# Windowed attention and a squared-ReLU MLP on one core: attention in pairs of PSUM banks, group 0's down-projection by products, merged stores, and a new order

## The chip, the cores and the metric

The kernel runs on one core of one Trainium2 chip. The metric is the time of one launch on the device in microseconds (us), the median of several runs of the same program. Engines are called as in the profile: PE (TensorE, matrix products), PEld (its weight loads, which run beside it), DVE (VectorE), ACT (ScalarE), POOL (GpSimd, which here only issues the loads) and SP (SyncE, which here only issues transfers). PSUM has eight banks of 128 x 512 float32.

## The reference

```python
def _attn_ref(q, k, v):                    # each (8, 8, 576, 64): batch, head, position, head size
    scores = scale * np.matmul(q, k.transpose(0, 1, 3, 2))
    rel = pos[:, None] - pos[None, :]
    slopes = 2.0 ** (-8.0 * (np.arange(H) + 1) / H)
    bias = slopes[:, None, None] * (-np.abs(rel))[None]
    mask = (rel >= 0) & (rel < 128)
    scores = np.where(mask, scores + bias[None], -1000000000.0)
    attn = softmax(scores)
    return np.matmul(attn, v)

x = attn_out.transpose(0, 2, 1, 3).reshape(4608, 512)
h = x @ w_in                               # (512, 2048)
r = np.maximum(h, 0.0)
return (r * r) @ w_out                     # (2048, 512), float32
```

So a query sees itself and at most 127 keys before it. The two matrix products of the MLP are nearly all of the arithmetic.

## The kernel before, in words

**Tokens.** The 4608 tokens are nine groups of 512 (g = 0 to 8). A group is made of four ranges of 128 tokens; a range is a block of 128 positions of one batch entry or, since 576 = 4 x 128 + 64, a pair of 64-token blocks of two batch entries. The order of the blocks is fixed in `seq` and `ranges`; the first eight blocks are the first blocks of the eight batch entries.

**Attention of a block m.** POOL issues the loads of k, q and v (128 KB each as they land in bf16, L522 and L527). k and q are transposed, by PE for the first eight blocks (L583), by a transfer issued on SP for the others (`kqT`, L568). PE makes the scores (task `s`, L642) into four PSUM banks of the ring "a". ACT takes the exponential of each bank (`e`, L669, 512 columns), DVE multiplies each by a table of exp(bias) with the mask in it (`m`, L677, L680, L684). PE multiplies by v (`pv`, L749) in two halves of four heads, each half in one bank of the same ring "a"; a column of ones beside v gives the sum of the row. DVE takes the reciprocal (`r`, L768) and multiplies (`n`, L777), for each half. The result is transposed into xT, by PE for the first eight blocks (L797), by a transfer on SP for the others (L784). The first four blocks (`lone`) add the bias by a matrix product with an identity instead (L697, L706) and have two exponentials of 512 (L714).

**MLP up.** For groups 0 to 5, PE makes h in pieces of one PSUM bank of the ring "h" (two banks): tasks `u` (L896) in groups 0 to 2 and `fc` (L914) in groups 3 to 5. A piece of group 0 is four feature blocks of 128 by 128 tokens, and there are four such sets, one for each range of tokens; the set of features names the part of w_in that it needs. Groups 6 to 8 use seven products of 256 columns instead of eight (task `f`, L995, Strassen's method in Winograd's form). ACT takes the ReLU into a ring "rt" (L857), DVE or ACT squares it into the bf16 tile g (L869, L867).

**MLP down.** Group 0 is done directly: for each range of 128 tokens, 16 matmuls of 512 columns (task `o`, L1071), evacuated by ACT or DVE and stored as 128 x 512. Groups 1 to 8 go by seven products of half size instead of eight (`product`, task `p` g.number.half, L1158): products 1 and 2 need only g and w_out; 5 and 6 need sums of quarters of g (`S1`, `S2`, made by DVE at L1281 out of the finished g) and of w_out (`wsum`, made once at L1114); 7, 3 and 4 need `S3` and `S4`. A group's four results are snapped or added into SBUF tiles "osb" (L376, L374, L1212, L1221, L1224) and stored by SP, each 128-token quarter-result by a transfer of its own (L1196), a pair of 64-token blocks by two. The last product of group 8 is cut up at the very end (`last_product`, L1241, L1251, L1258).

**The order.** All of it is tasks with a key (when it is wanted), candidate engines, dependencies, and rings of buffers that they take and give back. `Plan.order` lays them out once, when the program is built, with a table of costs, and every engine then runs its instructions in that fixed order; `ADJ` holds corrections of single keys. Where the plan foresees a gap on PE in the first 30 us, `fill` (L355) puts dummy matmuls there. The weights are loaded in pieces between the first blocks' loads (`FIRST`, w_in in five pieces of 2, 2, 4, 4 and 4 feature blocks, w_out in four).

Of the kernel before, what the change touches and what calls it, by code (L numbers as in the profile page):

```python
# [22 lines left out]
N_PVH = 2  # L23
# [15 lines left out]
G_STR = 1  # L39
G_A = 8  # L40
XR = 12
OSB = 5
# [6 lines left out]
RT = 4  # L49
# [80 lines left out]

class Slot:


    def __init__(self, tag):
        self.tag, self.tile, self.left, self.freed, self.idx, self.turn = tag, None, 0, 0.0, 0, 0


class Plan:


    LAT = {"PE": 210.0, "ACT": 180.0, "DVE": 190.0, "POOL": 200.0, "SP": 200.0, "ACTQ": 200.0}
    SELF = {"ACT": 120.0, "DVE": 110.0}
# [123 lines left out]
def kernel(  # L266
# [23 lines left out]
    for b in range(0, B, 2):  # L290
        for x in [(b + i, kb) for i in range(2) for kb in range(1, HALF)]:
            jobs.append(("full", [len(seq)]))
            seq.append(x)
            ranges.append([x])
        jobs.append(("half", [len(seq), len(seq) + 1]))
        seq += [(b, HALF), (b + 1, HALF)]

        ranges.insert(len(ranges) - (b + 2 == B), seq[-2:])
# [58 lines left out]
    def tile_of(slot):  # L357
        return tiles[slot.tag][slot.idx]

    def act(n):  # L360
        return n * 0.832 + 51.0
# [980 lines left out]
```

## Time and profile before

| | us |
|---|---|
| three runs | 301.82, 301.49, 300.56 |
| median of the runs | 301.49 |
| the profiled execution | 302.54 |
| its span (first to last instruction) | 300.8 |
| what lies around the span | 1.74 |
| PE busy / DVE / ACT / POOL | 288.8 / 243.3 / 205.2 / 106.5 |
| mean granted clock of PE | 0.994 |

The span is what the profile's rows add up to; the profiled execution is 1.05 us above the median of the runs. Busy times of one engine don't add up with another's: they run side by side. In the chain that ended last, PE has 85% of the span, a transfer of w_in 5%, POOL's issuing 5%, DVE 2%.

### The profile page before, as it was taken

How to read it: one execution, taken by the hardware profiler on the slowest of the kernel's cores; microseconds unless marked ns; L12 is line 12 of the kernel's file. 1: busy time of each engine (PE TensorE's matmuls, PEld its weight loads, DVE VectorE, ACT ScalarE, POOL GpSimd, SP SyncE). 2: the span in 40 equal slices, each digit the busy share in tenths (PEclk: the TensorE clock that was granted, in tenths of full speed). 3: DMA queues.
4: the chain of work that ended last, by engine and by line, in shares of the span. 5: the costliest groups of instructions: out<-in, count | busy, mean ns of one | idle time of the engine just before them, and what ended most of it. 6: DMA issues, size and time to landing. Idle time of an engine off the chain costs nothing.

```text
span 300.8 us, 8326 instructions
## 1 busy us (share of the span) xinstructions
PE 288.8 (96%) x3279; PEld 226.2 (75%) x3299; DVE 243.3 (81%) x628; ACT 205.2 (68%) x390; POOL 106.5 (35%) x132
## 2 busy tenths in 40 slices
PE   8799999997999999999999999999999999999992
PEld 4588757886888888556576776568888888888882
DVE  5567568679877899688799997699989998999852
ACT  2685445576487673785978747896979669888710
POOL 8944488445551585522639205510000000000000
PEclk9999999999799999999999999999999999999999
DMA  9999999999999999999999999996103101110213
GB/s 126 170 201 206 181 190 159 164 173 174 174 167 186 123 130 187 164 157 140 167 187 179 160 191 166 152 158 107 37 17 109 38 35 37 70 37 0 80 61 108
DMA packets 170920, 39.62 MB, mean 132 GB/s; under 512 B 156928, under 2 KB 170368, under 8 KB 170880
## 3 DMA queue, kind: packets, MB, share of 16 engines
q0 software_dynamic: 115184, 18.10, 86.5%
q1 hardware_dynamic: 55264, 20.66, 39.2%
q8 instruction: 26, 0.43, 0.6%
q10 hardware_dynamic: 432, 0.33, 0.4%
q14 instruction: 14, 0.11, 0.1%
HBM read 36.70 MB, written 9.44 MB: 153 GB/s over the span
## 4 chain that ended last, share of the span: by engine, by line
PE 85%; DMA 5%; POOL 5%; DVE 2%; issue 1%; POOLq 0%
PE o L1158 33%; PE h L914 14%; PE h L995 12%; PE h L896 10%; PE pv L749 6%; PE s L642 5%; DMA w_in_sb<-in_moe_w_in_dram 5%; PE o L1071 4%; POOL kq L522 2%; POOL vf L527 1%; POOL w_in_sb L467 1%; DVE sums L1281 1%; PE tp L583 1%; PE o L1241 1%; DVE g L869 1%
## 5 line engine op out<-in xcount | busy, mean ns | idle before, releaser
L857 ACT ACTIVATE rt<-h 128x512 bf16<-128x512 f32 (+1 forms) x109 | 64.4, 595 | 30.6 <-PE h L896 14.8
L669 ACT ACTIVATE P<-s 128x512 bf16<-128x512 f32 x120 | 63.6, 604 | 12.7 <-PE s L642 12.7
L1158 PEld LDWEIGHTS <-g 128*128 128x128 bf16 x624 | 59.5, 98 | 8.2
L869 DVE TENSOR_TENSOR g<-rt 128x512 bf16<-128x512 bf16 (+1 forms) x101 | 41.7, 415 | 20.1 <-ACT rt L857 18.6
L522 POOL DMA_DIRECT2D kq<-in_k_dram x39 | 33.2, 852 | 54.0 <-DMA kqT<-kq 47.4
L1158 PE MATMUL o<-w_out_sb,g 128*128 128x256 bf16 x384 | 47.2, 273 | 0.0
L896 PE MATMUL h<-xT,w_in_sb 128*128 128x128 bf16 (+1 forms) x512 | 46.6, 246 | 0.4 <-DMA w_in_sb<-in_moe_w_in_dram 0.4
L914 PE MATMUL h<-xT,w_in_sb 128*128 128x512 bf16 x178 | 45.0, 379 | 0.7
L896 PEld LDWEIGHTS <-w_in_sb 128*128 128x128 bf16 x512 | 38.6, 98 | 4.2 <-DMA w_in_sb<-in_moe_w_in_dram 0.6
L677 DVE TENSOR_TENSOR P<-P,masks 128x512 bf16<-128x512 bf16 x96 | 38.3, 416 | 3.1 <-ACT P L669 1.2
L527 POOL DMA_DIRECT2D vt<-in_v_dram x32 | 27.1, 855 | 31.5 <-PE pv L749 30.7
L522 POOL DMA_DIRECT2D kq<-in_q_dram x39 | 33.6, 862 | 7.7 <-PE h L896 3.2
L1158 PE MATMUL o<-wsum,sums 128*128 128x256 bf16 x256 | 32.9, 279 | 2.1 <-DVE sums L1281 2.1
L777 DVE TENSOR_TENSOR x<-pv,rec 128x256 bf16<-128x256 f32 (+1 forms) x80 | 31.7, 413 | 0.7
L1158 PE MATMUL o<-wsum,g 128*128 128x256 bf16 x240 | 30.7, 273 | 0.0
L1158 PEld LDWEIGHTS <-sums 128*128 128x128 bf16 x256 | 25.1, 100 | 6.6 <-DVE sums L1281 2.3
L914 PEld LDWEIGHTS <-w_in_sb 128*128 128x128 bf16 x192 | 17.2, 98 | 16.6
L749 PEld LDWEIGHTS <-P 128*128 128x128 bf16 (+1 forms) x576 | 23.7, 101 | 6.2 <-issue 0.9
L867 ACT ACTIVATE g<-rt 128x512 bf16<-128x512 bf16 x44 | 27.6, 629 | 1.1
L857 ACT ACTIVATE rt<-vf 128x512 bf16<-128x512 f32 x36 | 22.5, 626 | 6.2 <-DVE vf L1016 5.8
L1016 DVE TENSOR_TENSOR vf<-h,vf 128x512 f32<-128x512 f32 x36 | 24.2, 685 | 2.6 <-PE h L995 2.2
L376 ACT ACTIVATE osb<-o 128x512 f32<-128x512 f32 x21 | 12.6, 598 | 17.1 <-PE o L1158 14.8
(81 smaller groups left out, 393.5 us busy)
## 6 DMA issues: line engine op xcount, KB each, us to landing
out_dram<-osb SPq DMA_DIRECT2D x55, 128.0 KB, 2.7
kq<-in_k_dram POOLq DMA_DIRECT2D x31, 128.0 KB, 7.0
kq<-in_q_dram POOLq DMA_DIRECT2D x31, 128.0 KB, 7.5
vt<-in_v_dram POOLq DMA_DIRECT2D x24, 128.0 KB, 7.5
w_out_sb<-in_moe_w_out_dram POOLq DMA_DIRECT2D x4, 512.0 KB, 14.6
w_in_sb<-in_moe_w_in_dram POOLq DMA_DIRECT2D x3, 512.0 KB, 10.6
out_dram<-osb SPq DMA_DIRECT2D x17, 64.0 KB, 2.1
vf<-in_v_dram POOLq DMA_DIRECT2D x8, 128.0 KB, 6.9
```

The lines of the kernel that those rows point to most:

```text
L522: nc.gpsimd.dma_start(view(kq[s_kq[m].idx], i), source(src, m, split))
L527: nc.gpsimd.dma_start(tile_of(s_v[m])[0:n, :, 0:D], source(v, m))
L669: nc.scalar.activation(flat(Pt[sP.idx]), sS[i].tile.rearrange("p (j t) -> p j t", j=2)[:, :, lo:hi], AF.Exp, bias=0.0, scale=scale)
L677: nc.vector.tensor_tensor(flat(Pt[sP.idx]), flat(Pt[sP.idx]), flat(masks), op=ALU.mult)
L749: nc.tensor.matmul(sv.tile[0:n, hi * (D + 1):(hi + 1) * (D + 1)], prob, tile_of(s_v[mk])[:, h, 0:D + 1], start=mk == parts[0][1], stop=mk ...
L777: nc.vector.tensor_tensor(o, heads(sv)[0:n, :, 0:D], sr.tile[0:n, :].unsqueeze(2).to_broadcast([n, 4, D]), op=ALU.mult)
L857: nc.scalar.activation(srt.tile[:, 0:n], i, AF.Relu, bias=0.0, scale=1.0)
L869: nc.vector.tensor_tensor(o, i, i, op=ALU.mult)
L896: nc.tensor.matmul(slot.tile[:, f * w:(f + 1) * w], w_in_sb[:, cc, fc * 128:(fc + 1) * 128], xT[:, cc, lo % (XR * 128):lo % (XR * 128) + w ...
L914: nc.tensor.matmul(slot.tile, w_in_sb[:, cc, fc * 128:(fc + 1) * 128], xT[:, cc, g * 512 % (XR * 128):g * 512 % (XR * 128) + 512], start=c ...
L995: nc.tensor.matmul(slot.tile[:, j * 256:j * 256 + 256], a, b_, start=fresh and j == 0 and c == 0, stop=c == 1, skip_group_check=True)
L1158: nc.tensor.matmul(slot.tile[:, z * 256:z * 256 + 256], stationary(c), moving(c), start=fresh and z == 0 and c == 0, stop=c == F - 1, skip ...
```

## The change

What the diff does, part by part:

1. **Pairs of banks.** Ring "a" has two slots of two banks instead of four of one. A block's scores take both slots; there are two exponentials and two mask products of 1024 columns instead of four of 512. Both halves of `pv` go to one slot, with one reciprocal of 8 columns and one product of 512 columns instead of two of 4 and of 256 (from the fifth block on). A scores task also waits for the `pv` of the job two before (`t_last`).
2. **Group 0's down-projection by products.** `G_STR = 0`: 112 matmuls of 256 columns replace 64 of 512; four snaps or copies of 512 columns are joined by three DVE additions, and eight sums of 1024 columns (S1 to S4) are added on DVE. No first product can start before the whole up-projection of its half of the tokens, and product 2 needs all of the second half of w_out.
3. **Stores.** `places` joins the two 128-token quarters of a result in one transfer (128 x 2 x 256) where both are whole blocks, and a pair of 64-token blocks in one (2 x 64 x 256, the pair outermost on the DRAM side). In the last group the stores of the result `c12`, and of one of the pieces at the very end, are issued on ACT. The last pair of 64-token blocks moves from the second last range to the fourth last.
4. **Rings.** osb 4 instead of 5, rt 3 instead of 4. Slots of the first blocks' k, q and v are chosen by block.
5. **Order.** A new `ADJ`. In the program as built the order on the engines is another:

- POOL's first instructions are the loads of blocks 1 and 2 (k, q, k, q) and one load of v, then the iota, which was first. The weights' order was w_in 0, 1, 3, 2, then w_out 0, 2, w_in 4, w_out 1, (k and q of block 4), w_out 3. It is w_in 0, then blocks 3's k and q and two v, then w_in 2, w_out 2, w_in 4, 3, 1, w_out 0, 1, 3. In KB as landed, what is issued on POOL up to and with each: before, w_in 0 1408, w_in 3 2176, w_out 2 3840, w_in 4 4352, w_out 1 4864, w_out 3 5632; after, w_in 0 1024, w_in 2 2048, w_in 4 3072, w_in 1 (the last of w_in) 3840, w_out 1 4864, w_out 3 5376.
- PE's up-projection of group 0, in matmuls of 128 columns: before 8, 40, 64, 32, 48, 64 with eight matmuls of `o` after the first 144; after 8 (w_in 0), 64 (w_in 2), nine dummies, 64 (w_in 4), 16 (w_in 3), 56 (w_in 1), 48 (w_in 3), then products 1 and 2.
- The end of group 1's up-projection: before, its last matmuls were followed by the scores of block 10 and then product 5 (products 1 and 2 had been issued earlier); after, by product 1, the scores of block 10, product 2 and product 6.
- PE's dummies are 33 instead of 27. SP issues 43 stores instead of 76, ACT 3 instead of 1.

The diff without `ADJ`, cut to its core:

```diff
-G_STR = 1
+G_STR = 0
-OSB = 5
+OSB = 4
-RT = 4
+RT = 3
-        ranges.insert(len(ranges) - (b + 2 == B), seq[-2:])
+        ranges.insert(len(ranges) - 3 * (b + 2 == B), seq[-2:])
-    psum_bufs = {"h": 2, "ox": 1, "oy": 1, "a": 4}
+    psum_bufs = {"h": 2, "ox": 1, "oy": 1, "a": 2}
     def bank(slot, name):
-        slot.tile = psum.tile([128, 512], FP32, tag=slot.tag, bufs=psum_bufs[slot.tag], name=name)
+        slot.tile = psum.tile([128, 2, 512] if slot.tag == "a" else [128, 512], FP32, tag=slot.tag,
+                              bufs=psum_bufs[slot.tag], name=name)
...
-        sS = [Slot("a") for _ in range(4)]
+        sS = [Slot("a") for _ in range(2)]
...
-            deps = [last["s"]]
+            deps = [last["s"], t_last.get(j - 2)]
...
-        cols = 2 * (hi - lo)
-        for i in range(4):
-            w = slice(2 * i, 2 * i + 2)
+        cols = 4 * (hi - lo)
+        for i in range(2):
+            w = slice(4 * i, 4 * i + 4)
...
-                nc.scalar.activation(flat(Pt[sP.idx]), sS[i].tile.rearrange("p (j t) -> p j t", j=2)[:, :, lo:hi],
+                nc.scalar.activation(flat(Pt[sP.idx]),
+                                     sS[i].tile.rearrange("p r (j t) -> p (r j) t", j=2)[:, :, lo:hi],
                                      AF.Exp, bias=0.0, scale=scale)
...
+        pair = Slot("a") if j >= N_PVH else None
+        two = pair is not None and kind != "lone"
...
+            def norm():
+                nc.vector.tensor_tensor(
+                    xt[sx.idx][0:n, :].rearrange("p (b h e) -> p b h e", b=2, h=4), both()[:, :, :, 0:D],
+                    sr.tile[0:n].unsqueeze(3).to_broadcast([n, 2, 4, D]), op=ALU.mult)
+            t_n.append(plan.add({"DVE": dve_p(512)}, due - 11, norm, [t_r], [sx], [pair, sr], name=f"n{m}.0"))
...
+    def places(r, n):
+
+        rows = [[b * S + kb * 128 for b, kb in ranges[r + i]] for i in range(n)]
+        if n == 2 and len(rows[0]) == len(rows[1]) == 1:
+            lo, d = rows[0][0], rows[1][0] - rows[0][0]
+            if d >= 128 and lo + 2 * d <= NT:
+                return [((0, 1), lambda w: out[lo:lo + 2 * d, w].rearrange("(j p) c -> p j c", p=d)[0:128])]
+        to = []
+        for j, x in enumerate(rows):
+            if len(x) == 1:
+                to.append(((j,), lambda w, x=x: out[x[0]:x[0] + 128, w]))
+            else:
+                d = x[1] - x[0]
+                lo = x[0] + 64 - d
+                to.append(((j,), lambda w, lo=lo, d=d: out[lo:lo + 2 * d, w].rearrange("(h p) c -> h p c", p=d)[:, d - 64:d]))
+        return to
...
+            for i, (j, to) in enumerate(places(4 * g + tok, 2)):
+                def run(j=j, to=to):
+                    (nc.scalar if end else nc.sync).dma_start(
+                        to(w), so.tile.rearrange("p (j c) -> p j c", j=2)[:, j[0]] if len(j) == 1 else
+                        so.tile.rearrange("p (j c) -> p j c", j=2))
...
-            combine("s2", lambda o: nc.vector.tensor_tensor(o, slot.tile, o, op=ALU.add), both + [st["s2"]], [slot],
-                    0, 1, "c12")
+            combine("s2", lambda o: nc.vector.tensor_tensor(o, view(), o, op=ALU.add), both + [st["s2"]], [slot],
+                    0, 1, "c12", g == NG - 1)
...
+            q = z == 1 and lo == 0
+            def store(lo=lo, hi=hi, q=q):
+                to = places(4 * g + 2 + z, 1)[0][1]
+                (nc.scalar if q else nc.sync).dma_start(to(slice(lo, hi)), so.tile[:, z * 256 + lo:z * 256 + hi])
```

More of the change, by code (lines that the diff above doesn't have):

```diff
@@ L632, in scores @@
                 for g2 in grps:
-                    for r in range(2):
-                        bank(sS[2 * g2 + r], f"s{r}")
-                fill(t_s[grps[0]], sS[2 * grps[0]])
+                    bank(sS[g2], "s")
                 for g2 in grps:
@@ L691, in lone @@
     def lone(j, m, due):
[L693 removed]
+        sS = Slot("a")
         def biases():
+            bank(sS, "s")
             for r in range(2):
[L697 removed]
+                nc.tensor.matmul(sS.tile[:, r], ident,
                                  slopes[:, 4 * r:4 * r + 4].rearrange("p c q -> p (c q)"), start=True, stop=False)
[L699 removed]
+        t_b = plan.add({"PE": 2 * mm(512)}, due - 33, biases, t_slope[0] + t_slope[1] + [t_ident, last["s"]], [sS],
                        name=f"b{m}")
@@ L754, in values @@
             t_pv = plan.add({"PE": 4 * len(parts) * 30.0 + 30}, due - 12 + hf, pv,
-                            [last["pv"]] + (t_P[hf:hf + 1] if kind == "lone" else t_P[2 * hf:2 * hf + 2]) + [x for _, mk in parts for x in t_v[mk]],
-                            [sv], rel, name=f"pv{m}.{hf}")
+                            [last["pv"]] + t_P[hf:hf + 1] + [x for _, mk in parts for x in t_v[mk]],
+                            [] if pair and hf else [sv], rel, name=f"pv{m}.{hf}")
             last["pv"] = t_pv
@@ L777, in norm, with both, rec @@
                 nc.vector.tensor_tensor(
-                    o, heads(sv)[0:n, :, 0:D], sr.tile[0:n, :].unsqueeze(2).to_broadcast([n, 4, D]), op=ALU.mult)
+                    o, heads()[0:n, :, 0:D], sr.tile[0:n, 0].unsqueeze(2).to_broadcast([n, 4, D]), op=ALU.mult)
             t_n.append(plan.add({"DVE": dve_p(256)}, due - 12 + hf, norm, [t_r] + t_n, [] if hf else [sx],
                                 [sv, sr], name=f"n{m}.{hf}"))
+        t_last[j] = t_pvs[1]
+        if two:
+            sr = Slot("rec")
+            def both():
+                return pair.tile[0:n, :, 0:4 * (D + 1)].rearrange("p b (h e) -> p b h e", h=4)
+            def rec():
+                sr.tile = work.tile([128, 2, 4], FP32, tag="rec", bufs=4, name="rec")
+                nc.vector.reciprocal(sr.tile[0:n], both()[:, :, :, D])
+            t_r = plan.add({"DVE": 85.0}, due - 11, rec, t_pvs, [sr], name=f"r{m}.0")
+            def norm():
[3 more added lines that the diff above has]
+            t_n.append(plan.add({"DVE": dve_p(512)}, due - 11, norm, [t_r], [sx], [pair, sr], name=f"n{m}.0"))
         if m >= N_XP:
@@ L978, in up_product @@
             tag = "a" if g >= UP_A and u % 2 else "h"
-            st["X"], st["Y"], st["done"] = Slot(tag), Slot(tag), {"before": last.get("s5")}
+            st["X"] = Slot(tag)
+            st["Y"], st["done"] = st["X"] if tag == "a" else Slot(tag), {"before": last.get("s5")}
         X, Y, did = st["X"], st["Y"], st["done"]
@@ L982, in up_product, with view @@
         fresh = p in (1, 2, 5)
+        def view():
+            return slot.tile if X is not Y else slot.tile[:, int(p in (2, 5, 3))]
         def emit():
-            if p in (1, 2):
+            if p == 1 or p == 2 and X is not Y:
                 bank(slot, "h")
@@ L1002, in up_product @@
         tm = plan.add({"PE": 4 * mm(256)}, key, emit, deps + st["x"] + [g_first.get(g)],
-                      ([slot] if p in (1, 2) else []) + new, rel, name=f"f{g}.{u}.{p}")
+                      ([slot] if p == 1 or p == 2 and X is not Y else []) + new, rel, name=f"f{g}.{u}.{p}")
+        if p == 1:
+            did["first"] = tm
         g_first.setdefault(g, tm)
@@ L1182, in run, with store, combine @@
                 so.tile = work.tile([128, d_model], FP32, tag="osb", bufs=OSB, name="osb")
-                copy(t, so.tile, slot.tile)
+                copy(t, so.tile, view())
             t = plan.add({"ACT": act(512), "DVE": dve_p(512)}, key, run, both, [so], free, name=f"{name}_{g}")
             st[name] = t
-        def store(name, t, hi, tok, cols=(0, 512)):
+        def store(name, t, hi, tok, end=False):
             so = st["slot"][name]
-            for j in range(2):
-                if not cols[0] <= j * 256 < cols[1]:
-                    continue
-                def run(j=j):
-                    rows = [(b * S + kb * 128, i * 64, blk[kb]) for i, (b, kb) in enumerate(ranges[4 * g + tok + j])]
-                    for r, at_p, n in rows:
-                        nc.sync.dma_start(out[r:r + n, hi * 256:hi * 256 + 256],
-                                          so.tile[at_p:at_p + n, j * 256:j * 256 + 256])
-                plan.add({"SP": 530.0}, key, run, [t], [], [so], dma=340.0, lat=1000.0, name=f"st{g}.{p}.{tok + j}")
-        def combine(name, what, deps, free, tok, hi, label):
+            w = slice(hi * 256, hi * 256 + 256)
+            for i, (j, to) in enumerate(places(4 * g + tok, 2)):
[3 more added lines that the diff above has]
+                        so.tile.rearrange("p (j c) -> p j c", j=2))
+                plan.add({"ACTQ" if end else "SP": 530.0}, key, run, [t], [], [so], dma=340.0 * len(j), lat=1000.0,
+                         name=f"st{g}.{p}.{tok + i}")
+        def combine(name, what, deps, free, tok, hi, label, end=False):
             so = st["slot"][name]
@@ L1205, in combine @@
             t = plan.add({"DVE": dve_p(512)}, key, run, deps, [], free, name=f"{label}_{g}")
-            store(name, t, hi, tok)
+            store(name, t, hi, tok, end)
             return t
@@ L1234, in last_product, with emit @@
         for lo, hi in cuts:
-            slot = Slot("a")
-            end = z == 1 and hi == 256
-            def emit(slot=slot, lo=lo, hi=hi):
-                bank(slot, "o")
+            k = int(z == 0 or lo > 0)
+            if z == 0:
+                slot = st["slot"]["Y5"]
+            elif lo == 0:
+                slot = st["slot"]["E"] = Slot("a")
+            else:
+                slot = st["slot"]["E"]
+            def emit(slot=slot, lo=lo, hi=hi, k=k, z=z):
+                if z and not k:
+                    bank(slot, "o")
                 for c in range(F):
-                    nc.tensor.matmul(slot.tile[:, 0:hi - lo], stationary(c), wsum[:, 3, c, lo:hi],
+                    nc.tensor.matmul(slot.tile[:, k, 0:hi - lo], stationary(c), wsum[:, 3, c, lo:hi],
                                      start=c == 0, stop=c == F - 1)
```

114 lines of the change are left out of this document (63 added, 51 removed), and 106 rows, old and new, of the table ADJ.

## The prediction

> **What bounds the kernel now.** I read the busy times first, then who waited on PE, then the chain that ended last, then the stretches around the one long wait, then the timeline of SP at the end.
>
> The page, the span and the busy times:
>
> ```profile
> span 300.8 us, 8326 instructions
> ...
> PE 288.8 (96%) x3279; PEld 226.2 (75%) x3299; DVE 243.3 (81%) x628; ACT 205.2 (68%) x390; POOL 106.5 (35%) x132
> ```
>
> All that PE waited for (total, times, longest):
>
> ```profile
> PE o L1158 <- DVE sums L1281: 2.1, 1, 2.1
> PE wm L551 <- DVE sums L394: 1.2, 1, 1.2
> PE s L706 <- ACT kqf L376: 0.7, 1, 0.7
> PE pv L749 <- ACT kqf L376: 0.6, 1, 0.6
> PE h L896 <- DMA w_in_sb<-in_moe_w_in_dram: 0.4, 1, 0.4
> PE tp L583 <- ACT kqf L376: 0.2, 1, 0.2
> ```
>
> Pieces of the chain (start, us, what):
>
> ```profile
> 14.77 15.98 DMA w_in_sb<-in_moe_w_in_dram
> 30.79 3.75 PE h L896 x64
> ...
> 36.71 2.59 PE o L1071 x12
> ...
> 72.73 1.22 DVE sums L1281 x2
> ...
> 295.31 0.29 DVE osb L1251
> ```
>
> The stretches after that wait (stretch: its length, then busy PE, PEld, DVE, ACT, POOL with counts, granted clock):
>
> ```profile
> 72.00:73.00 1.00, 0.00 (x0) 0.00 (x0) 1.00 (x3) 1.00 (x3) 0.00 (x0) 1.00 1.72 174
> ...
> 75.00:76.00 1.00, 1.00 (x8) 0.76 (x6) 1.00 (x3) 0.00 (x0) 1.00 (x2) 0.58 1.44 211
> 76.00:77.00 1.00, 1.00 (x15) 0.59 (x15) 1.00 (x3) 0.45 (x1) 0.63 (x1) 0.50 1.29 210
> 77.00:78.00 1.00, 1.00 (x13) 0.64 (x8) 0.97 (x3) 1.00 (x3) 0.33 (x1) 0.50 1.99 227
> ```
>
> SP's stores at the end (start, us):
>
> ```profile
> 296.47 1.74 SPq L1258 DMA_DIRECT2D out_dram<-osb  x3
> ```
>
> PE is the bound: from 30.79 to 295.29 the chain is PE but for one place. At 71.9 PE waits 2.08 us for DVE's sums, DVE having been the chain from 67.17 to 73.95 without a pause, and then runs at half clock for three microseconds. The rest is the beginning (up to 30.8, set by when w_in lands) and the end: the last addition is done at 295.60, yet SP, behind with its stores, issues the last three from 296.47, and the span ends at 300.8. So an edit that only lightens ACT or DVE gains nothing unless PE waits for it; only these four things can move the time: PE's work, the place at 72, the beginning, the end.
>
> **The change part by part**, against the span of 300.8.
>
> *Group 0 by products.* Twelve matmuls of 512 columns take 2.59 us in the chain, 0.216 each; 16 of 256 take 1.75, 0.109 each. 64 x 0.216 = 13.8 becomes 112 x 0.109 = 12.25: **-1.6**. On DVE come eight sums (1.22 for two, 0.61 each) and three additions, 6.7 us in all, most of it between 30 and 60, where DVE is busy 6.4 to 7.2 of each 10 us; PE's other work covers them. Without that cover product 6 would wait for S2.
>
> *The beginning.* POOL's landings, by who waited for them: 1408 KB by 15.9 (w_in 0), 3840 by 28.3, 4352 by 30.75, 4864 by 33.3, 5632 by 37.6 (DVE's wsum waits), about 200 KB per us. Without the iota ahead everything starts 0.5 earlier (first load at 1.34, iota from 0.84). By the KB of the new order: w_in 2 at 15.9 + 640/196 - 0.5 = 18.7; w_in 4 at 23.9; w_in 3 at 26.5; w_in 1 at 27.8; w_out 1 at 32.8; w_out 3 at 35.7. Before, PE had by 18.7 some 32 of the 256 matmuls of the up-projection behind it (17.39 onwards), now eight. Then 64 x 0.056 and a transposition end at 22.6, PE waits 1.3 for w_in 4, and the remaining 184 (10.3 us) end at 34.2. Before, it was 34.4 with eight matmuls of `o` (1.7) already done. Net **+1.5**. Products 1 then last until 35.95, and product 2 finds w_out 3 landed at 35.7. Bounds: 0, if the loads come 1.5 us earlier than so read (PE is then dense as before); +3.9, if the wait grows to 2 us and halves the clock as at 72. I take 1.5, since at 0.4 to 1.2 us (the other waits in PE's list) the granted clock stayed at 1.00.
>
> The Trainium skill (TensorE: Matmul & The Clock Gate, What's actually happening) has the clock halve after an idle window of about 3.4 us; here 2.08 us were enough, so the measurement decides. By the page's figure the wait for w_in 4 would cost its 1.3 and no more, which is also what I take.
>
> *The wait at 72.* It costs 2.08, and the slow clock 0.77 (16 matmuls 2.52 instead of 1.75), 0.42 (scores 0.97 instead of 0.55) and 0.66 (eight matmuls 1.53 instead of 0.87): 3.9 in all. In the new order, between group 1's last up-projection and the first product that takes sums lie product 1 (1.75), scores (0.55) and product 2 (1.75), 4.05 us. DVE must by then have done, after ReLU (0.2 + 0.6 + 0.1), two squares (0.33 each), S1, a memset and S2 (0.61 each): 2.9. DVE's own queue: from the mask of block 8 to that S2 I count two masks each for blocks 8 and 9, seven squares, two reciprocals and products, five sums and two memsets at these prices, 10.2 us; PE's work from the scores of block 8 to product 6 is 14.3, and the masks can begin 1.9 after its start: 12.1 against 14.3. So the wait goes: **-3.9**, and what is late next is nothing, with 1 to 2 us to spare. Bounds: 0 to -3.9.
>
> *Pairs.* Two masks of 0.33 become one of about 0.61, two products of 0.33 one of 0.61, a reciprocal of 0.1 is saved for each block: some 8 us of DVE, and about 0.07 of ACT for each pair. All of it lies beside PE: **0**. But an exponential now holds ACT twice as long (four of 512 take 2.07, so 1.0 instead of 0.52), a ReLU behind it is up to 0.5 later, and the two banks of "h" come free later. PE waited for ACT nowhere after 31 us, so nearest is 0; the other end is 60 x 0.5 = 30. A gain below 0 is excluded but through the place at 72. I take one exposed: **+0.5**. Slots of two banks come back whole: scores wait for two exponentials and the product, where PE has 1.75 to 2.6 us of other work in the orders I looked at; in the same +0.5. The new wait on `pv` of the job two before stands behind work that PE has done in its own order anyhow: 0.
>
> *Stores, rings, order.* 33 issues fewer on SP free x and kqT transfers from waiting behind stores; PE doesn't wait for those: 0. At the end SP now has one of z = 0 and one last store, while `c12` and the middle piece go on ACT, idle then, with nothing behind them; the moved pair makes the last pieces whole blocks, one transfer each. Last addition as before 0.3 after the last matmul, issue 0.2 later, landing 1.9 (this line's median): 2.4 after the matmul, against 297.7 + 1.9 - 295.3 = 4.3: **-1.9**. Bounds: -1.9 and, if a merged store lands as slowly as this kernel's slowest store (8.3 us), +2.3: `c12` is added 1.0 before the last matmul's end and would land 7.4 after it. I take the near one, as all stores of the last 15 us landed in 1.7 to 2.6. Rings of 4 and 3: 0, covered by DVE's relief; a square that is late would hold ReLU and then PE.
>
> Sum: -1.6 + 1.5 - 3.9 + 0.5 - 1.9 = -5.4. The profiled execution is 302.54, so 297.1; its ratio 0.982 on the median of 301.49 gives **296.1**.
>
> **The rivals.**
>
> *A. A pair's store is slow.* The 2 x 64 x 256 store has 2 outermost. If it runs on two DMA engines instead of 16, its 128 rows of 1 KB are 64 on each; the hardware queue's 1472 packets took 24.3% of 16 engines over the last 16 us, 42 ns each, so 2.7 us instead of 0.3. `c12`'s store, issued 0.9 before the last matmul's end, then lands 3.3 to 3.9 after it, not 2.4: about 1.2 of the gain goes, **297.3**. For it: two outer rows can't be dealt to 16; against it: no store here has that shape.
> The Trainium skill states this (DMA: Bandwidth & Descriptors, Why a DMA increments its semaphore by 16 and not by 1): the number of engines is the largest up to 16 that divides both sides' slowest dimension, here 2. No run here shows it yet.
>
> *B. The beginning halves the clock.* The wait for w_in 4 reaches 2 us: + 0.7 and + 1.8, **298.6**. For it: the landings are read to about 0.7 us only.
>
> *C. The wait at 72 stays or moves to another group.* DVE is busy 19.7 and 19.8 of 20 us in 160 to 180 and 200 to 220, so a late sum can hit PE there; two microseconds cost 3.9 with the clock: **300.0**.
>
> *D. Slower: ReLU behind long exponentials.* ACT in order, 1.0 us at a time, two "h" banks that fill in 0.87 each, one place less in "rt". Each exposed exponential costs 0.5; it decides from 11 of the 60 on (5.4 / 0.5), and with 16 more, 8 us, it is **304**. For it: ReLU and the next fill leave no slack (0.2 + 0.6 against 0.87); against it: 33 waits of ACT for PE's `h`, 14.8 us, say that ACT is the earlier.
>
> **How the numbers follow.** Forecast 0.45, A 0.18, B 0.10, C 0.12, D 0.15. 0.5% (1.5 us) is about what a measurement of this kernel can tell from no change. Faster are the forecast, A, B and half of C: 0.78; the same is the rest of C and a mild D: 0.09; slower 0.13. The range runs from 293.3 (no new wait, no loss in the beginning, a little from DVE) to 301.5; it leaves out most of D and a small share below.
>
> **What would show it.** PE's list without the wait for L1281's line and a granted clock of 1.00 from 70 to 80; the first product of group 0 at about 34; a wait for w_in 4 near 23; the last store 2 to 4 us after the last matmul; exponentials of 1.0 us. Wrong it would be by ACT's ReLU or an "h" wait in PE's list many times over, by a new wait of 2 us or more, or by landings later than read.

## The result, and the profile after

The change makes the kernel slower: 314.45 us (median of four, 312.53 to 317.32) against 301.02 (300.54 to 301.82), a ratio of 1.042, 95% interval 1.034 to 1.051. The prediction was 296.1, range 293.3 to 301.5. The profiled execution took 315.91, its span is 314.1: 13.3 more than the span before, where the prediction's sum was -5.4. The ratio leaves out the execution of 317.32, which is slower than the fastest of the four by more than 1.5%. Executions of the changed kernel differ by more than those before do, so small effects are read from the traces, stretch by stretch.

The page of the changed kernel, span and busy times:

```profile
span 314.1 us, 8252 instructions
...
PE 292.8 (93%) x3353; PEld 230.9 (74%) x3353; DVE 236.5 (75%) x503; ACT 204.0 (65%) x334; POOL 106.3 (34%) x132
```

DVE has 7 us less to do, as forecast, and PE is busy longer, though its matmuls are shorter in sum: a large part of the difference is slow clock, half speed from 9 to 12 and from 118 to 125, where the kernel before had it only from 75 to 79. What PE waited for (total, times, longest):

```profile
PE h L935 <- DMA xT<-x: 3.7, 1, 3.7
PE h L1020 <- DVE vf L1043: 2.8, 7, 0.6
PE s L693 <- ACT sums L430: 1.4, 1, 1.4
PE wm L547 <- DVE sums L390: 1.2, 1, 1.2
PE h L1020 <- DVE vf L370: 1.0, 2, 0.5
PE o L1207 <- ACT osb L372: 0.7, 1, 0.7
...
PE h L917 <- ACT rt L878: 0.5, 2, 0.3
```

The wait for sums at 72 is gone. In its place stand a wait for a transposition of x (`xT`), nine for DVE in the up-projection of the last groups, and one for `osb`. ReLU behind long exponentials (rival D) is the last line shown: 0.5 us in two waits, both before 32. The stretches (length, then busy PE, PEld, DVE, ACT, POOL with counts, granted clock, share of the DMA engines, GB/s):

```profile
70.00:80.00 10.00, 10.00 (x136) 8.62 (x135) 9.91 (x20) 4.44 (x6) 4.23 (x6) 1.00 2.10 148
110.00:120.00 10.00, 6.30 (x91) 5.41 (x89) 5.74 (x11) 1.65 (x3) 4.70 (x6) 0.91 2.01 155
120.00:130.00 10.00, 10.00 (x61) 5.10 (x60) 3.85 (x8) 5.12 (x8) 4.01 (x5) 0.75 1.75 194
240.00:255.00 15.00, 13.21 (x118) 11.23 (x117) 12.78 (x24) 10.25 (x18) 0.00 (x0) 1.00 0.17 34
```

70 to 80 is dense at full clock, as predicted. PE stands still for 3.7 us before 120 and then runs at half clock until 125; in the kernel before, 120 to 140 had a clock of 1.00. And from 240 on PE has holes where it had none. The chain of waits there (start, us, what):

```profile
108.27 3.61 PE o L1207 x33
111.88 7.80 DMA xT<-x
119.68 0.04 issue
119.72 3.57 PE h L935 x8
```

And the stores at the end, on the queues of ACT and SP (start, us):

```profile
306.70 1.54 ACTq L1245 DMA_DIRECT2D out_dram<-osb  x2
...
308.34 0.38 ACTq L1316 DMA_DIRECT2D out_dram<-osb  x1
```

```profile
307.02 1.07 SPq L1316 DMA_DIRECT2D out_dram<-osb  x2
```

Everything is issued by 308.7, the last matmul ends at 306.8, and yet the span ends at 314.1.

**A balance by stretches.** To find where 13.3 us went I took, at each point of PE's order, the time elapsed less the matmuls issued so far, each at the distance that its form has when nothing is in the way (0.216 us for 512 columns, 0.109 for 256, 0.056 for 128, 0.029 for a `pv` of 65). The remainder is what PE has lost up to there, and two kernels can be compared although their orders differ. It still grows after 78 in the kernel before, where PE waits for nothing, so it holds time that these distances do not price; only differences between kernels are read from it. And a wait costs PE some 0.16 more here than in PE's list, which counts from the modelled end of the matmul ahead: 0.27 after its start for 256 columns, where the next can start after 0.109.

| up to | loss before | loss after | added in this stretch |
|---|---|---|---|
| end of group 0's up-projection (35) | 7.6 | 10.2 | +2.6 |
| 69 | 9.4 | 12.2 | +0.2 |
| 78 | 13.4 | 13.1 | -3.1 |
| 103 | 15.9 | 15.4 | -0.2 |
| 137 | 18.6 | 24.1 | +6.0 |
| 239 | 26.1 | 32.0 | +0.4 |
| last matmul | 26.2 | 39.0 | +6.9 |
| matmuls themselves | 268.9 | 267.7 | -1.2 |
| from the last matmul to the end | 5.5 | 7.3 | +1.8 |

Sum +13.4. Four places are to be explained: groups 7 and 8 (+6.9), the stall before group 3 (+6.0), the tail (+1.8, forecast -1.9), the beginning (+2.6, forecast +1.5).

### The profile page after: what moved, and what is told of

Read it like the earlier page. It is cut to its first block, busy times and chain, and to the rows that moved or that the text cites. A ratio compares the mean times of both kernels' runs of the same rounds, so it can differ in the third digit from the quotient of the medians.

```text
span 314.1 us, 8252 instructions
## 1 busy us (share of the span) xinstructions
PE 292.8 (93%) x3353; PEld 230.9 (74%) x3353; DVE 236.5 (75%) x503; ACT 204.0 (65%) x334; POOL 106.3 (34%) x132
## 4 chain that ended last, share of the span: by engine, by line
PE 76%; DVE 10%; ACT 5%; DMA 2%; issue 2%; POOL 2%; DVEq 0%; POOLq 0%; ACTq 0%
PE o L1207 29%; PE h L935 13%; PE h L917 13%; PE h L1020 8%; PE pv L754 5%; PE s L636 5%; DVE vf L1043 3%; DMA xT<-x 2%; ACT rt L878 2%; DVE vf L370 1%; DVE sums L1341 1%; POOL kq L518 1%; PE tp L579 1%; DVE g L1341 1%; ACT masks L410 1%
## 5 line engine op out<-in xcount | busy, mean ns | idle before, releaser
L1207 PEld LDWEIGHTS <-g 128*128 128x128 bf16 x704 | 67.8, 98 | 11.8 <-issue 1.4
L663 ACT ACTIVATE P<-s 128x1024 bf16<-128x1024 f32 x60 | 59.1, 1022 | 16.9 <-PE s L636 16.9
L890 DVE TENSOR_TENSOR g<-rt 128x512 bf16<-128x512 bf16 (+1 forms) x101 | 40.9, 414 | 22.0 <-ACT rt L878 21.5
L1207 PE MATMUL o<-w_out_sb,g 128*128 128x256 bf16 x432 | 52.1, 273 | 0.7 <-ACT osb L372 0.7
L935 PE MATMUL h<-xT,w_in_sb 128*128 128x512 bf16 x192 | 48.9, 390 | 3.7 <-DMA xT<-x 3.7
L672 DVE TENSOR_TENSOR P<-P,masks 128x1024 bf16<-128x1024 bf16 x48 | 32.4, 686 | 7.8 <-ACT P L663 7.8
L1207 PE MATMUL o<-wsum,sums 128*128 128x256 bf16 x288 | 35.7, 273 | 0.0
L1207 PE MATMUL o<-wsum,g 128*128 128x256 bf16 x272 | 35.7, 277 | 0.0
L1207 PEld LDWEIGHTS <-sums 128*128 128x128 bf16 x288 | 27.7, 98 | 4.3
L1043 DVE TENSOR_TENSOR vf<-h,vf 128x512 f32<-128x512 f32 x36 | 24.1, 683 | 2.9 <-PE h L1020 2.4
L798 DVE TENSOR_TENSOR x<-pv,rec 128x512 bf16<-128x512 f32 (+1 forms) x36 | 24.6, 685 | 0.6
L372 ACT ACTIVATE osb<-o 128x512 f32<-128x512 f32 x22 | 13.1, 597 | 15.3 <-PE o L1207 11.5
```

The lines of the kernel that those rows point to most:

```text
L663: nc.scalar.activation(flat(Pt[sP.idx]), sS[i].tile.rearrange("p r (j t) -> p (r j) t", j=2)[:, :, lo:hi], AF.Exp, bias=0.0, scale=scale)
L672: nc.vector.tensor_tensor(flat(Pt[sP.idx]), flat(Pt[sP.idx]), flat(masks), op=ALU.mult)
L890: nc.vector.tensor_tensor(o, i, i, op=ALU.mult)
L935: nc.tensor.matmul(slot.tile, w_in_sb[:, cc, fc * 128:(fc + 1) * 128], xT[:, cc, g * 512 % (XR * 128):g * 512 % (XR * 128) + 512], start=c ...
L1043: t = plan.add({"DVE": dve_p(512)}, key, lambda: nc.vector.tensor_tensor(cs[so.idx], view(), cs[so.idx], op=ALU.add), [tm, did[of]], [], [ ...
L1207: nc.tensor.matmul(view()[:, z * 256:z * 256 + 256], stationary(c), moving(c), start=fresh and z == 0 and c == 0, stop=c == F - 1, skip_gr ...
```

## The experiments

Each time is a median beside runs of the kernel before on the same chip, whose median was 300.4 to 301.7. The edits are shortened; lines in plain words say what moves.

**Groups 7 and 8: a tile of two banks.** Odd units of the up-projection have their two halves X and Y in the two banks of one pair. Product 6 accumulates into X and needs ACT's copy of X; DVE at the same time adds to Y's product. The changed kernel, one unit's beginning (start, us, engine, line, instruction, idle time before it and what ended it):

```profile
247.53 0.60 ACT L372 ACTIVATE vf<-h 128x512 f32<-128x512 f32 x1
...
248.22 0.68 DVE L1043 TENSOR_TENSOR vf<-h,vf 128x512 f32<-128x512 f32 x1
...
248.95 0.60 PE L1020 MATMUL h<-ut,kqf 128*128 128x256 bf16 x4 [0.59 <-DVE vf L1043]
...
250.46 1.29 DVE L370 COPY vf<-h 128x512 f32<-128x512 f32 x2 [1.23 <-PE h L1020]
...
251.80 1.03 PE L1020 MATMUL h<-xT,w_in_sb 128*128 128x256 bf16 x8 [0.51 <-DVE vf L370]
```

The copy that product 6 needs is done at 248.13; the product starts at 248.95, when the addition to the *other* half ends (248.90). Product 7 needs the first of the two copies at 250.46 and starts when the second ends (251.75). As built, the program orders accesses by tile, and the tile is now both banks.

```diff
-            slot.tile = psum.tile([128, 2, 512], FP32, tag="a", bufs=2)      # from group 7 on
+            slot.tile = [singles.tile([128, 512], FP32, tag="b", bufs=4) for _ in range(2)]
```

> The changed kernel, with the same order on every engine; from group 7 on the two halves of a pair are two tiles of one bank each instead of one tile of two banks. Theory (a wait between the halves): in the changed kernel product 6 of an odd unit begins when DVE's addition to the other half ends (248.95, addition until 248.90), not when its own copy is done (248.12), and the same holds for products 7, 3 and 4 and for products 2 and 6 of group 8. From 239 to the last matmul PE loses 7.0 us against its matmuls' own durations; that should fall to 1 to 2, and the time from 314.4 to 308 to 309.5. Rival (the order: too little other work stands between the links of the chain 1, copy, 6, copy, 7): the order is unchanged, so the waits stay, and the time is 313 to 315.

Measured: 307.3 us, ratio 1.017 (1.009 to 1.025). What PE waited for in this kernel, and its stretches from 240:

```profile
PE h L946 <- DMA xT<-x: 3.6, 1, 3.6
PE s L704 <- ACT sums L441: 1.4, 1, 1.4
...
PE h L1031 <- DVE vf L1054: 0.4, 1, 0.4
```

```profile
240.00:255.00 15.00, 15.00 (x139) 13.43 (x138) 13.93 (x26) 11.78 (x22) 0.00 (x0) 1.00 0.16 31
255.00:270.00 15.00, 15.00 (x140) 13.44 (x138) 14.19 (x25) 10.48 (x19) 0.00 (x0) 1.00 0.16 54
```

L1054 is the line that was L1043. Of its seven waits the one of 0.4 at 214, ahead of group 7, is left; those for the copy and the one for `osb` (products 1 and 2 of group 8 shared a pair too) are gone, and from 245 to the last matmul the loss does not move (31.0 throughout, against 32.0 to 39.0). The order on every engine was the same, so the rival, the order, is excluded.

**The stall before group 3.** SP's timeline in the changed kernel (start, us):

```profile
91.95 12.51 SPq L564 DMA_TRANSPOSE kqT<-kq  x3
104.55 1.28 SPq L805 DMA_TRANSPOSE xT<-x  x1
106.00 3.17 SPq L564 DMA_TRANSPOSE kqT<-kq  x1
109.26 5.01 SPq L805 DMA_TRANSPOSE xT<-x  x3
```

Three transpositions of k and q held SP for 12.5 us, about half of it waiting for their loads, and x13 waited behind them although DVE had finished block 13's rows at 96.1. The loads were late: q of block 18 landed 14.1 us after its issue, in the kernel before 5.0. In the kernel before, x13 went out at 93.1, ahead of kqT18. The first experiment moves the four x forward on SP and nothing else:

```diff
     done = plan.order()
+    put("kqT18", behind="x13"); put("kqT19", behind="kqT18"); put("kqT20", behind="x16")
```

> The changed kernel; on SP alone the transposition x13 is issued before those of kqT18 and kqT19, and x14 to x16 before kqT20; nothing else moves. Theory (SP's order): SP stood from 91.95 to 104.5 at kqT17 to kqT19, whose k and q had not landed, with x13 ready at about 96.5 behind them; x16 was then issued at 111.9 to 114.3 and landed at 119.7. With the new places x16 goes out at 106 to 108 and lands by 115.8, group 3's first product starts at 115.8 to 116.5 instead of 119.7, the granted clock stays at 1.00, and 3.9 + 1.8 us go: 308.5 to 310. Rival (the transfers themselves are slow, 6 to 8 us from issue to landing among larger stores): the landing moves little, 2 us or more of the stall and the halved clock stay, 312 to 314.5.

Measured: 312.6, ratio 1.038 (1.034 to 1.042). Group 3 starts at 115.6 without a wait, as the theory said, but only 2 of the 6 us are gained, since another transposition is late instead. PE's list:

```profile
PE h L1020 <- DVE vf L1043: 2.8, 7, 0.6
PE s L636 <- DMA kqT<-kq: 2.0, 2, 1.8
```

The wait for kqT stands at 131, and the clock halves behind it. So SP's order decides which transfer is late, not whether one is. Four more runs ask why.

```diff
-SIZE = {"kq": 4, ...}      # buffers for k and q as loaded
+SIZE = {"kq": 6, ...}      # the order on all queues kept
```

> The changed kernel with six buffers for k and q as loaded instead of four, every queue in the same order; a load then no longer waits for the transposition of the block four before, which POOL did for 66.5 us in all. Theory (the loads are bound by this round trip, 8 us to land and 8 to transpose): loads of blocks 17 to 20 go out 3 to 10 us earlier, SP no longer stands at kqT18 and kqT19, x16 is issued by 107, the stall of 3.7 us before group 3 and the slow clock go: 308 to 309.5. Rival (the transfers themselves are the limit, the two queues together holding the DMA engines for more than the whole time): more loads in flight land later, the stall stays within 2 us of what it was, 312 to 315.

Measured: 319.8 (315.5 to 321.9), slower than the changed kernel by 3 to 5 us. No wait is left before group 3, but one of 2.7 us, with a slow clock behind it, stands at 80.9 for `xT`, and another of 2.6 at 198.1, where `pv` waits for its masked probabilities. The theory fails in its time; the run does not settle the round trip, since PE reached group 3 late (120.2) through what it lost at 81. x16 was issued at 109.8, not by 107, and q of block 18, issued 4.1 earlier, landed only 2.8 earlier.

```diff
                 def run(j=j, to=to):
+                    if g < 3:
+                        return
```

> The changed kernel without the stores of groups 0 to 2 (their results are left out), so that up to 160 us only loads and transpositions use the DMA engines. Theory (SP's order and the round trip of the loads): stores are 1 to 2 us of SP's time in this stretch, the stall before group 3 shrinks by at most 2 us, 311 to 314. Rival (stores of 256 KB get in the way of the transpositions): the stall goes, 308 to 309.

Measured: 310.9 (1.032, 1.026 to 1.038), two executions, although the beginning of the traced one was 1.5 us worse. From 33 to 209 the trace has no pause above 0.25 us: without these bytes the stall is gone. q of block 18 landed 6.8 us after its issue instead of 14.1, and x16 was issued at 105.4 instead of 111.9, so it is more than PE's late beginning.

```diff
-                    (nc.scalar if end else nc.sync).dma_start(
+                    (nc.scalar if end or g < 3 else nc.sync).dma_start(
```

> The changed kernel with the stores of groups 0 to 2 issued on ACT's queue instead of SP's; the same bytes move. Theory (the stores are in the way on SP and on its queue, where transpositions stand behind them): the stall before group 3 goes as it did without these stores, 308 to 311. Rival (the stores' bytes on the DMA engines are what is in the way): the stall stays, 313 to 316.

Measured: 316.6 (1.051, 1.045 to 1.056): the wait for `xT` is 3.6, in the changed kernel 3.7. So neither SP's time for the stores nor standing behind a store on SP's queue is the cause.

```diff
-  return [((0, 1), lambda w: out[lo:lo + 2 * d, w].rearrange("(j p) c -> p j c", p=d)[0:128])]
+  return [((0, 1), lambda w: [out[lo + d * h:lo + d * h + 128, w] for h in range(2)])]
```

> The changed kernel with its stores of 128 x 2 x 256 sent as two of 128 x 256, as before the change, on the same queues. Theory (merging is what holds up the transpositions at 105 to 120: 256 KB at a time on the queue): the stall before group 3 goes, 308 to 310. Rival (merging makes no difference; the order on SP, x13 to x16 behind three kqT whose loads are late, does): the stall stays, 313.5 to 316.

Measured: 313.0 (1.039, 1.036 to 1.043); the profiled execution, the slowest of its five, has a stall of 5.0. Merging the stores is not the cause; whether it adds a microsecond stays open.

What these runs show: from about 75 to 135 loads, transpositions and stores together leave the transfers no slack in this order. Fewer bytes remove the stall; another queue for the same bytes, or two stores for one, do not; with more buffers for loads or another order on SP a wait stands elsewhere. Why the same bytes leave slack in the order of the kernel before stays open.

**The tail.** Pairs of 64-token blocks go by one transfer of 2 x 64 x 256 in the changed kernel. The bytes that the queues moved from 306 to 315 (40 slices, GB/s):

```profile
GB/s 382 205 0 0 0 0 0 0 9 141 332 128 59 61 27 36 50 89 159 341 346 216 66 46 46 46 46 50 36 0 0 0 0 0 0 0 0 0 0 0
```

Twice it falls to some 60 GB/s and below, the second time until 312.5. The edit sends such a pair as two transfers again:

```diff
-  out[lo:lo + 2 * d, w].rearrange("(h p) c -> h p c", p=d)[:, d - 64:d]
+  [out[lo + d * h + d - 64:lo + d * h + d, w] for h in range(2)]      # two dma_start
```

> The changed kernel, with the pairs of 64-token blocks stored by two transfers of 64 x 256 as before the change, on the same queues; stores of 128 x 2 x 256 stay merged. Theory (the 2 x 64 x 256 transfer is slow by itself): after 301 and after 307 the queues move only 42 to 49 GB/s for about 3 us each; with two transfers the span ends 4.5 to 5.2 us after the last matmul instead of 7.3, and the time is 312 to 312.5. Rival (ACT as issuer, or the number of stores at the end, is what costs): the tail stays at 6.5 to 7.3 us, 314 to 314.5.

The same view of that kernel:

```profile
GB/s 27 346 391 364 37 0 0 0 0 0 5 168 191 305 251 260 321 367 235 205 25 0 0 0 0 0 0 0 0 0 0 0 0 0 0 0 0 0 0 0
```

The slow tail is gone; the span ends 4.85 us after the last matmul instead of 7.3, with the same issuers. The time, 314.0, hides it, since the stall before group 3 was 4.9 in the profiled execution; one of its four executions took 307.3, of which there is no trace.

**The beginning.**

```diff
     done = plan.order()
+    put("iota", first on POOL)
```

> The changed kernel, with the iota first on POOL as before the change. Theory (slopes late): PE waited 1.4 us at 6.9 for the slopes, which need the iota, so the first matmul of the up-projection moves from 18.1 to 16.6 to 17.2, and the up-projection of group 0 ends near 34.7 instead of 35.8: 313 to 313.5. Rival (the loads set the beginning): every load goes out 0.5 later, the wait for the slopes is replaced by a later one for k, q or w_in, and the up-projection ends at 35.8 to 36.3: 314.5 to 315.

Measured: 315.9 (1.047, 1.041 to 1.054). The loss at the end of group 0's up-projection is 8.6, against 9.2 to 9.6 in the traces of the two tiles, of SP's order and of the split stores: 0.6 to 1.0 gained, so the theory holds for this stretch. The wait for the slopes itself stays, 1.3 against 1.4, only 0.7 earlier. The gain is lost again: PE waits 1.7 at 80 and 2.0 at 117, both for `xT`.

**Together.**

```diff
+ two tiles from group 7 on;  SP's places of x13 to x16;  pairs of 64-token blocks by two transfers
```

> The changed kernel with three edits together: two tiles of one bank from group 7 on, SP's places of x13 to x16, and pairs of 64-token blocks stored by two transfers. Theory (three separate losses that add): against the changed kernel's 314.4, 7.0 for the banks, 1.8 as measured for SP's places, 2.4 for the tail: 303.2, so still slower than the kernel before by 0.5 to 1%. Rival (they overlap, and what one gives back another takes, as the transposition of kqT took the place of x's): 305 to 308.

Measured: 300.86 (0.999, 0.996 to 1.002): the three repairs give 13.6 us together, 2.3 more than the sum expected, and the changed kernel is level with the one before. The 2.3 is within the spread of the changed kernel's executions. In the trace, of the fastest of ten, the span ends 4.0 after the last matmul, and 1.7 us of wait for kqT is left at 131; no slow clock followed.

> The three edits of the run before last with six buffers for k and q. If the round trip of the loads is what is late, both stalls (before group 3, and at the scores that took its place) are gone: 300 to 301, within 0.5% of the kernel before. If the transfers are the limit, 303 to 305.

Measured: 303.1 (1.007, 1.003 to 1.010). Again the stall moves to 81, 3.7 us for `xT`, this time without a slow clock behind it (1.00 from 84 to 88).

> The three edits together (two tiles from group 7 on, SP's places of x13 to x16, pairs of 64-token blocks by two transfers), which gave 300.9, with the iota first on POOL. Theory (as its own run showed, the up-projection of group 0 ends 0.6 us earlier): 300.2 to 300.5. Rival (what the beginning gains comes back as a wait for a transposition between 75 and 135): 300.9 to 303.

Measured: 300.98 (1.001, 0.998 to 1.004). The median gains nothing, as the rival has it, but the trace, of the fastest of ten, does not show the rival's mechanism: the loss at 34 is 8.9, the wait for kqT only 0.7, the span 298.0. What takes the gain in the others stays open.

**The place at 72 alone, in the kernel before.** Does it pay, or do transfers take it back there too?

```diff
-  PE: p1.2 p1.1 (most of) s8 xp7 ... u1.1.5 s10 p1.5 s11 p1.6
+  PE: s8 xp7 ... u1.1.5 p1.1 s10 p1.2 p1.6 s11 p1.5
```

> The kernel before, where only the place at 72 is changed: group 1's products 1 and 2 are moved behind the last matmuls of its up-projection and product 6 ahead of product 5, as in the changed kernel; DVE's and ACT's work on them follows. Theory (the wait at 72 stands for itself): its 2.1 us and the slow clock go, 297 to 298. Rival (the transfers between 75 and 130 have no slack, and the wait covered them): PE comes 3 to 4 us sooner to group 3 and to the scores around 105 to 130, waits there for xT or kqT, 2 us or more with a slow clock behind them, and the time is 300 to 302.

> The kernel of the run before with the two stores of the last group's c12 on ACT's queue instead of SP's. Theory (SP is behind with its stores at the end): SP's last three go out 0.8 us earlier, the span ends 4.5 to 4.8 us after the last matmul instead of 5.5, 0.7 to 1.0 us below the run before. Rival (a transfer's landing sets the end, not its issue): no difference.

Measured: 309.8 and 309.1. Inconclusive: I had placed the store of c11 ahead of the addition to it, the addition waited for the store to land, and PE waited 5.5 us for the addition. (The second run has only the queue of c12's stores in addition; its tail was 4.4 us, against 5.1.) Placed anew:

> The kernel before, where only the place at 72 is changed, placed anew: in the first try the store of group 1's c11 stood ahead of the addition that it should carry, which then waited 5.5 us for that store to land (and a quarter of group 1's output lacked product 2); now the store follows the addition, and the copy for it on ACT follows the last ReLU. Theory (the wait at 72 stands for itself): 297 to 298.5. Rival (the transfers between 75 and 130 have no slack, and the wait covered them): PE comes 2 to 4 us sooner to group 3 and to the scores around 105 to 130, waits there for xT or kqT, 2 us or more with a slow clock behind them, and the time is 300 to 302.

> The kernel of the run before with the two stores of the last group's c12 on ACT's queue instead of SP's. In the first try this ended the span 4.4 us after the last matmul instead of 5.1. Theory: the same again, 0.7 us below the run before. Rival (another execution's landing is as late): no difference.

Measured: 300.84 (0.998, 0.995 to 1.001) and 300.09 (0.996, 0.994 to 0.998). PE comes earlier to 111 (a loss of 15.5, against 16.8 before) and no transfer stalls it, so the kernel before has the slack that the changed one lacks; the rival's mechanism falls. But the theory's time is missed too: without the move of the stores the gain is 0.5, and its interval includes no change. The ten executions (300.6 to 301.1) lie where those of the kernel before with a mean clock above 0.994 lie (median 300.62 of 13 beside them; the other ten 302.28). Two waits of PE's own were left (0.5 at 59, 1.2 at 76.7); the last edit is meant to remove both:

```diff
+  PE: p1.1.0 stays ahead of s8;   ACT: exponentials of block 11 ahead of the copies of products 6 and 5
```

> The kernel before with the place at 72 changed and c12's stores on ACT, as in the run before last but one edit better: group 1's product 1 stays half where it was, so that the wait of 0.7 us at 58.9 is filled, and the exponentials of block 11 stand ahead of the copies of products 6 and 5 on ACT, so that pv of block 10 finds its bank 1.3 us sooner. Theory (these two waits, 2.0 us together, are PE's own): 298.0 to 298.8. Rival (the transfers take it back further on): 299.5 to 300.5.

Measured: 299.42 beside 300.43, ratio 0.997 (0.994 to 1.000). Its page and what PE waited for:

```profile
span 297.1 us, 8326 instructions
...
PE 287.5 (97%) x3279; PEld 225.1 (76%) x3299; DVE 242.8 (82%) x627; ACT 205.7 (69%) x391; POOL 106.4 (36%) x132
```

```profile
PE wm L551 <- DVE sums L394: 1.2, 1, 1.2
PE s L706 <- ACT kqf L376: 0.9, 1, 0.9
PE pv L749 <- ACT kqf L376: 0.6, 1, 0.6
PE h L896 <- DVE xT L374: 0.5, 1, 0.5
PE o L1158 <- DVE g L869: 0.5, 1, 0.5
```

The wait at 76.7 is gone but for 0.2; at 59 to 61 there are now two of 0.5. The time misses the theory (298.0 to 298.8) and, against its own runs of the kernel before, is no better than the edit ahead of it. These two kernels, both with c12's stores on ACT, lie lowest against the kernel before, by 0.3 to 0.4%: the interval of the edit ahead excludes no change, that of the last edit just includes it.

## Why the prediction was wrong, step by step

- **Group 0 by products (-1.6): right.** Matmuls by 1.2 less, which is 1.6 less for group 0 and six dummies of 0.056 more. DVE's eight sums stayed covered; PE's list has no wait for them of 0.5 us or more.
- **The beginning (+1.5): size nearly right by luck, mechanism wrong.** +2.6 in the profiled execution, +1.6 to +2.0 in three other traces with the same beginning. The landings were read well (w_in 4 at 24.0, forecast 23.9), but the forecast wait for w_in 4 did not come, since PE was later than its loads. "Without the iota ahead everything starts 0.5 earlier" left out who needs the iota: the slopes came late, PE waited 1.4 for them, and the first matmul of the up-projection stood at 18.1 (17.1 in the three others) instead of 15.9. In the profiled execution the clock was also 0.77 from 10 to 15; with the iota behind the loads five of ten traces have such a fall between 8 and 18 us, with it first none of eight.
- **The wait at 72 (-3.9): it went, but its price was that of one execution.** The stretch gained 3.1. The profiled execution before had a mean clock of 0.994 and 302.54 us; of 79 executions of the kernel before, 29 had 0.994 or less, with a median of 302.05, the other 50 had 300.59. That fits a slow clock behind the wait, 1.85 of the 3.9, about once in three; where the clock fell in these executions no trace shows. Taking the place out of the kernel before gave 0.5 in the median alone and 1.0 to 1.3 with c12's stores, not 3.9. "What is late next is nothing" was wrong for this kernel.
- **Pairs (+0.5): the step that failed most, +6.9.** For the attention it was right: exponentials of 1.02 us, no wait for them, 0.5 for ReLU. But "Slots of two banks come back whole" was thought through for scores only. The diff makes X and Y of an odd up-projection unit in groups 7 and 8, and X and Y2 of group 8, halves of one tile, and a wait on one half became a wait on both: eleven waits of 0.2 to 0.7 us from 240 on, none of which is left with two tiles.
- **Stores and order on SP ("PE doesn't wait for those: 0"): +6.0.** I counted issues and did not follow SP's new order against the loads: x13 stands behind kqT18 and kqT19, x14 to x16 behind kqT20, and these three were issued only 11 to 15 us after the loads of their blocks. With x13 to x16 put ahead a wait of 1.8 came elsewhere, and without the stores of groups 0 to 2 the stall went: what failed is the 0 for PE's waits on transfers. A transposition that is late by 4 us costs PE 3.7 and a slow clock.
- **The tail (-1.9): +1.8, rival A.** The mechanism of A was as written; its size was not, 7.3 us after the last matmul instead of 3.3 to 3.9, because the addition of c12 ended 0.16 us before the last matmul and not 0.9, its issue on ACT took 1.1, and the queues moved some 50 GB/s for about 3 us. The Trainium skill (DMA: Bandwidth & Descriptors, Why a DMA increments its semaphore by 16 and not by 1) gives the number of engines by the slowest dimension, here 2; the runs agree, 46 GB/s being about what two engines with packets of 1 KB in 42 ns come to (49), while the queues moved 168 to 367 with two transfers of 64 rows. The far bound was summed wrongly: a landing 7.4 after the last matmul is 3.1 more than 4.3, not 2.3; +1.8 lies inside it.
- **Rings (0): right** as far as seen; the wait for `osb` in group 8 came from the shared pair.

Rivals: A happened. B did not as written (the clock fell in the beginning of some executions, before w_in 4). C named the right kind of loss, a wait that moves, but looked for it on DVE. D, the slower case, named the wrong mechanism. The chances for faster add up to 0.79, not 0.78.

## What to carry to other kernels

When buffers are merged, list who else uses the ring: a pair that suits one operation's length makes two independent halves wait for each other wherever a program tracks accesses by tile, and the waits that the built program carries should show it without a run, which was not tried here. An in-order queue of transfers must be read against the landings of what it waits for, not by its number of issues. Price a wait from several executions: a slow clock behind it may be there only in some, and then removing the wait gains little in the median.

## What the hardware showed that I had not expected

How long PE waits does not settle whether its clock halves. A wait of 1.8 at 131 halved it in one kernel (first line) and one of 1.7 at the same place did not in another (second):

```profile
134.00:135.00 1.00, 1.00 (x4) 0.33 (x3) 0.61 (x1) 1.00 (x2) 1.00 (x2) 0.50 1.47 199
```

```profile
134.00:135.00 1.00, 1.00 (x16) 0.64 (x15) 0.78 (x2) 1.00 (x2) 1.00 (x2) 1.00 1.27 283
```

The Trainium skill (TensorE: Matmul & The Clock Gate, What's actually happening) gives an idle window of about 3.4 us; these waits are shorter, so the measurement decides. Of the waits of 1.7 to 2.7 us after the first 33 us in the traces of the changed kernels and of the kernel before, those of 2.1, 1.8 and 2.7 halved it, those of 1.7, 1.7, 2.0 and 2.6 did not, and neither did the 3.7 at 81. And transpositions slow down beside loads: in the kernel before, at 99 us with POOL's queue silent, a packet of 256 bytes took 18 ns and 923 of them went in a microsecond; in the changed kernel from 109 to 112, with POOL's queue running, it took 31 ns and some 400 went (31 ns at 109 in the kernel before, too). That six buffers for k and q, meant to help, cost 3 to 5 us fits this, but was not shown to come from it.
